# Nine q blocks turned between the layers' groups instead of on TensorE, half of the score columns, and 18 decoding steps moved to GpSimd

## The chip, the cores and the metric

The kernel runs on one core of a Trainium2 chip. The metric is the device time of one launch in microseconds, as the median of several runs. The engines that compute are TensorE (matrix products and transposes, in the profile PE for the products and PEld for the loads of its weights), VectorE (DVE), ScalarE (ACT) and GpSimd (POOL). SyncE (SP) issues nearly all DMAs. Each engine works through its own instructions in order.

## What is computed

The reference, cut to what matters: an attention over 49 agents, and behind it two feed-forward layers, for 12480 tokens of 128 channels.

```python
def sm(a, b):
    s = scale * (a @ b.transpose(0, 2, 1))
    s = s - s.max(-1, keepdims=True)
    e = np.exp(s)
    return e / (e.sum(-1, keepdims=True) + 1e-09)
agent_v = sm(agents, k) @ v              # 49 x 128
x = sm(q, agents) @ agent_v              # 12480 x 128
h = x @ w_in;   g = h * (1.0 / (1.0 + np.exp(-h)));   x = g @ w_out      # 128 -> 2048 -> 128
h = x @ w2_in;  g = h * np.cos(h);                    x = g @ w2_out     # 128 -> 2048 -> 128
```

q, k, v and the agents are float32. The four weights are float64 and are read as pairs of 32-bit words, from which the kernel builds a high and a low part of each weight itself.

## The kernel before

The program has two parts.

**The attention** works on 13 blocks of k, q and v (12 of 1024 tokens, one of 192). A long string, `ORDER`, lists its steps one by one; each engine takes its own instructions in that order, so the string fixes the order on every engine. A step's name is two letters and a block. For a k block: `kT` (eight 128x128 transposes on TensorE), `kX` (copy by ScalarE), `kS` (scores, with TensorE's columns split into two halves of 64), `kM` (a maximum on VectorE). For a v block: `vt` (transposes of the scores), `vc` (copy), `va` (product with v, columns split again). For a q block: `qT`, `qX` (turned, copied), `qS` (eight score products, one for each 128 tokens), `qM`, `qB`, `qE`, `qZ`, `qR` (maximum, subtraction, exponential, sum, reciprocal), `qN` (GpSimd multiplies by the reciprocal), `qP`, `qK`, `qL` (GpSimd packs the probabilities, 49 columns each, as high part, low part and 30 columns more of the high part into 128 columns), `qt` (TensorE turns the packed tile, four 128x128 transposes for each half block) and `qk` (ScalarE copies the turned half block into its place `pT`). The right operand of `qS` holds the 49 agents twice, so each product has 98 columns, of which the next product overwrites the second 49.

Beside this run the 16 pieces of the weights' decoding. For each piece: `dA` and `dH` on ScalarE, and `d0`, `d1`, `d2`, `d3`, `d4`, `dL` on VectorE. `d4` subtracts the high part from the value, `dL` adds the rest and writes the low part; both read two 128x512 tiles in SBUF. A second string, `LOADS`, gives the order in which SyncE issues the loads of k, q, v and the weights' pieces; a load is issued when a buffer of its kind is free (five for k and q, three for v, three for w).

At the end of the attention, when the last `va` is done, `c0` to `c6`, `cA`, `ch`, `cw`, `cP`, `cl`, `cH` and `cs` multiply the agents' values into the first layer's weights, so that the layers read the turned probabilities `pT` directly. A third string, `FIRST`, orders what is left over beside the first five groups of the first layer (`LR`, `Lh`, `La`, `Lg`, `Ll`, `Ly`). In it `wy8` is eight products on TensorE whose result is not used.

**The layers** work on 25 tiles of 512 tokens (the last three are shorter), and on four groups of 512 hidden units for each tile. One turn of the loop over `g` issues group `g` of the first layer and group `q = g - 5` of the second. On TensorE a group takes the products of `L1_rest` and `L1_h` (hidden units), `L1_y`, `L2_h` and `L2_y`. VectorE takes `L1_lo`, `L2_r`, `L2_g` and `L2_hi` in each turn; in addition `L1_end_b` where `g % 4` is 0 and the output's transpose `L2_end` where it is 2. GpSimd takes `L2_lo` alone. `L1_rest_in` loads 19 rows of `pT` four times over, one turn of four ahead of their use.

Of the kernel before, what the change touches and what calls it, by code (L numbers as in the profile page):

```python
# [31 lines left out]
LINE = 32  # L32

# [24 lines left out]
cH2 qN11 LR0 cl1 Lh0.0 cs3 dA14 Lh0.1 qP11 cH1 La0.0 qK11 qL11 cw1 cs2 Lg0.0 qK12 cs1 qL12 La0.1 wy8 qt12.0  # L58
Ll0.0 LR1 Lg0.1 Lh1.0 d213 Lh1.1 d014 Ly0.0 La1.0 Ll0.1 Lg1.0 d114 LR2 Lh2.0 La1.1 d313 Lh2.1 Ll1.0 Ly0.1 dH14
Lg1.1 d214 Ly1.0 d413 La2.0 Ll1.1 qk12.0 Lg2.0 LR3 d314 Lh3.0 Ly1.1 La2.1 Ll2.0 Lg2.1 d115 Ly2.0 La3.0 Ll2.1  # L60
Lh3.1 Lg3.0 qt11.0 dL13 d414 LR4 La3.1 Lh4.0 Ll3.0 Ly2.1 dH15 Lg3.1 d215 Lh4.1 d315 Ly3.0 La4.0 Ll3.1 Lg4.0 d415
Ly3.1 La4.1 Ll4.0 dL15 qk11.0 Le3 qt11.1 Lf3 qk11.1 dL14
# [3 lines left out]
w0 k0 k1 k2 w1 k3 k4 k5 w2 q0 k6 w3 k7 k8 w4 q1 k10 w5 k9 q2 k12 k11 w6 v1 q3 v0 q4 w7 q5 q10 q6 w8 q8 q7 v3 q9  # L66
w9 w10 v2 v4 w11 v5 q12 v6 q11 w12 v9 v7 v10 w13 v8 v11 v12 w15 w14
# [4 lines left out]
def agent_attention_moe_moe_kernel(ctx, tc, q, k, v, agents, w_in, w_out, w2_in, w2_out, out):  # L72
# [17 lines left out]
    agT = const.tile([128, 2, NA], F32, name="agT")  # L90
# [10 lines left out]
    const.tile([128, LINE - 8], F32, name="fill")  # L101
# [46 lines left out]

    whole = ctx.enter_context(ExitStack())
# [16 lines left out]
    if True:  # L166
# [27 lines left out]
        def load(key, S):  # L194
# [53 lines left out]
        for j in range(2):  # L248
            nc.vector.tensor_copy(out=agT[:, j, :], in_=pa[:, :NA])
# [122 lines left out]
        def qS(S):  # L372
# [4 lines left out]
            ag2 = agT.rearrange("p j a -> p (j a)")  # L377
# [570 lines left out]
```

## Time and profile before

| | |
|---|---|
| median of 3 runs | 1080.2 us (1079.47 to 1080.25) |
| span of the profiled execution, first to last instruction | 1076.8 us |
| the profiled execution's own time | not listed apart; the runs' median lies 3.4 us above its span |
| busy: PE, PEld, DVE, ACT, POOL | 1065.2, 841.2, 964.1, 909.8, 504.0 us |
| mean granted TensorE clock | 0.999 |

The page divides the span into 40 slices and gives for each engine the busy share of a slice. Busy time of PE is not PE at its peak: matrix products are pipelined and their ends are modelled. Which work sets the end is read from the chain that ended last, stretch by stretch; what an engine that is not in the chain has left is read from the windows.

### The profile page before, as it was taken

The numbers are of one execution on the slowest core, as the hardware profiler recorded it, in microseconds if no ns is written. First come the engines' busy times: TensorE is split into PE (matmuls) and PEld (weight loads), VectorE is DVE, ScalarE is ACT, GpSimd is POOL, SyncE is SP. The second block draws the span as 40 slices with busy tenths as digits, with TensorE's granted clock in tenths as the row PEclk, the third lists the DMA queues.
The fourth block names the chain that finished last, engine by engine and source line by source line (L and its number), as shares of the span: only waits on it lengthen the run. The fifth ranks groups of instructions, "written<-read, shape, count | busy, mean of one in ns | idle before, by whom it ended". The sixth has DMA issues, their size and how long they took to land.

```text
span 1076.8 us, 14174 instructions
## 1 busy us (share of the span) xinstructions
PE 1065.2 (99%) x5267; PEld 841.2 (78%) x5267; DVE 964.1 (90%) x1067; ACT 909.8 (84%) x972; POOL 504.0 (47%) x264
## 2 busy tenths in 40 slices
PE   9999999999999999999999999999999999999997
PEld 5897777777777777777777777777777777788996
DVE  7877999989999999999989998999999999999897
ACT  5888988888888888888888888888888888888876
POOL 0445044554455445544554455445544554455555
PEclk9999999999999999999999999999999999999999
DMA  9963000000000000000000000000000000000000
GB/s 345 344 226 125 9 6 11 6 16 13 4 16 16 1 17 16 1 16 17 10 6 16 12 5 16 13 4 16 17 1 16 16 1 15 15 11 5 12 9 15
DMA packets 66221, 38.68 MB, mean 36 GB/s; under 512 B 52523, under 2 KB 57184, under 8 KB 66152
## 3 DMA queue, kind: packets, MB, share of 16 engines
q1 hardware_dynamic: 65352, 37.68, 11.5%
q8 instruction: 41, 0.67, 0.3%
q14 instruction: 28, 0.23, 0.1%
q10 hardware_dynamic: 800, 0.10, 0.1%
HBM read 27.58 MB, written 6.39 MB: 32 GB/s over the span
## 4 chain that ended last, share of the span: by engine, by line
PE 95%; DVE 2%; ACT 1%; POOL 1%; DMA 1%; issue 1%; SPq 0%; POOLq 0%; DVEq 0%; ACTq 0%
PE y L733 16%; PE y L737 16%; PE y L734 16%; PE h L701 10%; PE h L775 8%; PE h L777 8%; PE h L776 8%; PE h L689 4%; PE h L267 2%; PE h L379 2%; PE h L303 1%; PE y L366 1%; PE y L440 1%; POOL g2l L834 1%; DMA kraw<-in_k_dram 1%; DVE g L816 1%
## 5 line engine op out<-in xcount | busy, mean ns | idle before, releaser
L834 POOL TENSOR_TENSOR g2l<-g,g2h 128x1024 fp32r<-128x1024 f32 (+2 forms) x200 | 465.5, 2349 | 498.7 <-DVE g1l L724 489.0
L799 DVE SCALAR_TENSOR_TENSOR n<-n,h 128x1024 f32<-128x1024 int32 (+3 forms) x202 | 239.0, 1184 | 63.9 <-ACT n L789 50.8
L789 ACT ACTIVATE n<-h,quarter 128x1024 int32<-128x1024 f32 (+3 forms) x202 | 219.8, 1088 | 88.7 <-PE h L777 88.6
L724 DVE TENSOR_TENSOR g1l<-g,g1h 128x1024 fp32r<-128x1024 f32 (+2 forms) x200 | 239.7, 1199 | 9.7 <-ACT g1h L716 4.1
L816 DVE TENSOR_TENSOR g<-n,h 128x1024 f32<-128x1024 f32 (+3 forms) x202 | 238.0, 1179 | 4.0 <-ACT n L808 0.7
L709 ACT ACTIVATE g<-h 128x1024 f32<-128x1024 f32 (+2 forms) x200 | 199.4, 997 | 36.2 <-PE h L701 36.0
L808 ACT ACTIVATE n<-n,halfpi 128x1024 f32<-128x1024 f32 (+3 forms) x202 | 225.6, 1119 | 0.8 <-DVE n L799 0.8
L716 ACT CAST g1h<-g 128x1024 fp32r<-128x1024 f32 (+2 forms) x200 | 204.9, 1025 | 3.2
L825 DVE CAST g2h<-g 128x1024 fp32r<-128x1024 f32 (+2 forms) x196 | 155.5, 794 | 7.5
L733 PE MATMUL y<-g1h,o1h 128*128 128x512 f32 (+2 forms) x400 | 156.4, 391 | 0.1
L733 PE MATMUL y<-g2h,o2h 128*128 128x512 f32 (+2 forms) x400 | 154.9, 387 | 1.1 <-DVE o L856 0.9
L775 PE MATMUL h<-x2h,i2h 128*128 128x512 f32 (+2 forms) x400 | 154.2, 386 | 1.0 <-DVE g L816 1.0
L734 PE MATMUL y<-g2h,o2l 128*128 128x512 f32 (+2 forms) x400 | 154.5, 386 | 0.0
L734 PE MATMUL y<-g1h,o1l 128*128 128x512 f32 (+2 forms) x400 | 154.0, 385 | 0.0
L777 PE MATMUL h<-x2l,i2h 128*128 128x512 f32 (+2 forms) x400 | 153.9, 385 | 0.0
L776 PE MATMUL h<-x2h,i2l 128*128 128x512 f32 (+2 forms) x400 | 153.9, 385 | 0.0
L701 PE MATMUL h<-pT,w2h 128*128 128x512 f32 (+2 forms) x400 | 132.3, 413 | 0.0
L737 PE MATMUL y<-g2l,o2h 128*128 128x512 f32 (+2 forms) x400 | 122.3, 387 | 1.9 <-POOL g2l L834 1.9
L737 PE MATMUL y<-g1l,o1h 128*128 128x512 f32 (+2 forms) x400 | 121.2, 384 | 0.0
L733 PEld LDWEIGHTS y<-g1h,o1h 128*128 128x128 f32 x400 | 75.1, 188 | 21.1 <-DVE x2l L762 7.8
L701 PEld LDWEIGHTS h<-pT,w2h 128*128 128x128 f32 x400 | 67.3, 188 | 30.9 <-issue 23.9
L737 PEld LDWEIGHTS y<-g2l,o2h 128*128 128x128 f32 x400 | 74.9, 188 | 17.7 <-POOL g2l L834 3.1
(140 smaller groups left out, 1092.5 us busy)
## 6 DMA issues: line engine op xcount, KB each, us to landing
qraw<-in_q_dram SPq DMA_DIRECT2D x12, 512.0 KB
vraw<-in_v_dram SPq DMA_DIRECT2D x12, 512.0 KB
kraw<-in_k_dram SPq DMA_DIRECT2D x11, 512.0 KB
out_dram<-o SPq DMA_DIRECT2D x88, 64.0 KB
wraw<-in_moe_w_in_dram SPq DMA_DIRECT2D x8, 512.0 KB
wraw<-in_moe_w_out_dram SPq DMA_DIRECT2D x8, 512.0 KB
x<-pT SPq DMA_DIRECT2D x88, 38.0 KB
kraw<-in_k_dram SPq DMA_DIRECT2D x2, 256.0 KB
```

The source lines that it names most:

```text
L701: nc.tensor.matmul(out=h1s[g, k][:, j, :toks(t)], lhsT=w2h[:, 128 * c:128 * c + 128], rhs=x, start=False, stop=True)
L724: i = v.tensor_tensor(out=gl, in0=f, in1=b32(gh), op=ALU.subtract)
L733: nc.tensor.matmul(out=y, lhsT=wh[:, c, :], rhs=gh[:, j, :], start=(c == 0), stop=False)
L734: nc.tensor.matmul(out=y, lhsT=wl[:, c, :], rhs=gh[:, j, :], start=False, stop=False)
L737: nc.tensor.matmul(out=y, lhsT=wh[:, c, :], rhs=gl[:, j, :], start=False, stop=(c == NCH - 1))
L775: nc.tensor.matmul(out=y, lhsT=i2h[:, c, :], rhs=xh, start=True, stop=False)
L776: nc.tensor.matmul(out=y, lhsT=i2l[:, c, :], rhs=xh, start=False, stop=False)
L777: nc.tensor.matmul(out=y, lhsT=i2h[:, c, :], rhs=xl, start=False, stop=True)
L799: v.scalar_tensor_tensor(out=b32(n)[:, p], in0=n[:, p], scalar=-2.0 * PI, in1=h2s[g, k][:, p], op0=ALU.mult, op1=ALU.add)
L808: sc.activation(out=r[:, p], in_=r[:, p], func=AF.Sin, bias=halfpi)
L816: v.tensor_tensor(out=f[:, p], in0=r[:, p], in1=h[:, p], op=ALU.mult)
L834: i = (v if (g, k) == (NG - 1, 1) else gp).tensor_tensor(out=gl[:, p], in0=f[:, p], in1=b32(gh)[:, p], op=ALU.subtract)
```

## The change

Five things are changed.

1. In the attention, q blocks 2 to 10 end with `qN`, which now writes its result into a place of its own, `stash` (free places of later `pT` tiles). Their steps `qP`, `qK`, `qL`, `qt` and `qk` are gone.
2. For these blocks the layers' loop does the same work two tiles ahead of use, for each tile of 512 tokens: GpSimd packs half a block (`P_hi` where `g % 4` is 0, `P_lo` where it is 1), VectorE transposes its 32x32 squares (`P_turn`, where `g % 4` is 3), and five DMAs put the squares in their places by way of a buffer in HBM. The tokens of these tiles come in another sequence, so the q loads of the nine blocks become four DMAs of 32 partitions each, and the output DMAs write accordingly.
3. `qS` multiplies 64 tokens at a time by the 49 agents, held once: 16 products of 49 columns on the two halves of TensorE's columns in place of 8 of 98.
4. Ten `d4` (written `e4`) and eight `dL` (`eL`) go from VectorE to GpSimd.
5. `ORDER`, `FIRST` and `LOADS` are new throughout; `wy8` is gone, and the loads begin with k block 6.

```diff
+LATE = (2, 3, 4, 5, 6, 7, 8, 9, 10)
+HOME = {2: 8, 3: 9, 4: 10, 5: 0, 6: 1, 7: 2, 8: 3, 9: 4, 10: 0}
+STASH = {2: (2, 0), 5: (2, 1), 3: (3, 0), 6: (3, 1), 4: (4, 0), 7: (4, 1), 8: (5, 0), 9: (5, 1), 10: (6, 0)}
+STAGE = 7
...
-dA0 d00 d10 kT0 wm3 d20 dH0 d30 kX0 d40 kT1 dL0 kS0 kX1 kT2 kM0 dA1 kS1 kX2 d01 d11 kT3 kM1 dH1 kS2 d21 kX3 d31
...
+kT6 dA0 kX6 d00 d10 kT0 wm3 d20 dH0 kS6 d30 kX0 e40 kT10 kM6 dL0 kS0 kX10 kT8 dA1 kM0 d01 kS10 kX8 d11 d21 kT1 dH1 d31
...
-    agT = const.tile([128, 2, NA], F32, name="agT")
+    agT = const.tile([128, NA], F32, name="agT")
...
+            if key == "q" and S in LATE:
+                src = q[0, blocks[S][0]:blocks[S][0] + 1024, :].rearrange("(x i a s) c -> a i x (s c)", x=2, i=32, s=4)
+                for a in range(4):
+                    nc.sync.dma_start(
+                        out=t[32 * a:32 * a + 32].rearrange("i (x s) c -> i x (s c)", x=2), in_=src[a]
+                    )
+                return t
...
-                nc.tensor.matmul(
-                    out=ps[:p, NA * i:NA * i + 2 * NA], lhsT=xt[:, i // h, p * (i % h):p * (i % h) + p], rhs=ag2,
-                    start=True, stop=True,
-                )
+                for x in range(0, p, 64):
+                    w = min(64, p - x)
+                    at = p * (i % h) + x
+                    nc.tensor.matmul(
+                        out=ps[x:x + w, NA * i:NA * i + NA], lhsT=xt[:, i // h, at:at + w], rhs=agT,
+                        start=True, stop=True, tile_position=(0, x),
+                    )
...
-            nc.gpsimd.tensor_tensor(out=e, in0=e, in1=z.unsqueeze(2).to_broadcast([p, n, NA]), op=ALU.mult)
+            nc.gpsimd.tensor_tensor(out=stash(S) if S in LATE else e, in0=e, in1=z.unsqueeze(2).to_broadcast([p, n, NA]), op=ALU.mult)
...
+            e4=lambda S: d4(S, nc.gpsimd), eL=lambda S: dL(S, nc.gpsimd),
...
+        def P_hi(t, after_op):
+            if not half(t):
+                return
+            e, pk = late_in(t)
+            i = gp.tensor_copy(out=pk[:, :, 0:NA], in_=e)
+            tc.add_manual_dep(i.ins, after_op.ins.name, AFTER, reason="one at a time on the port to SBUF")
+            gp.tensor_copy(out=pk[:, :, 2 * NA:128], in_=e[:, :, 0:MORE])
+
+        def P_lo(t, after_op):
+            if not half(t):
+                return
+            e, pk = late_in(t)
+            i = gp.tensor_tensor(out=pk[:, :, NA:2 * NA], in0=e, in1=b32(pk)[:, :, 0:NA], op=ALU.subtract)
+            tc.add_manual_dep(i.ins, after_op.ins.name, AFTER, reason="one at a time on the port to SBUF")
+
+        def P_turn(t):
+            if not half(t):
+                return
+            v.transpose(
+                out=b32(stage(1)).rearrange("p (x s i) -> p s x i", x=4, i=32),
+                in_=b32(stage(0)).rearrange("p (s x i) -> p s x i", x=4, i=32),
+            )
+            d = scratch.tile([128, 4, 128], F32, tag="turned", name="turned")
+            nc.sync.dma_start(out=d, in_=b32(stage(1)).rearrange("p (x c) -> p x c", x=4))
+            for x in range(4):
+                nc.sync.dma_start(
+                    out=b32(pT(WIDE * t, WIDE))[32 * x:32 * x + 32, :].rearrange("j (a c) -> j a c", a=4),
+                    in_=d[:, x, :].rearrange("(a j) c -> j a c", j=32),
+                )
...
-            L2_hi(q - 1, 0)
+            hi = L2_hi(q - 1, 0)
             L1_h(g, 0)
+            if g % 4 == 0:
+                P_hi(g // 4 + 2, hi)
+            if g % 4 == 1:
+                P_lo(g // 4 + 2, hi)
...
             L2_n(q, 1)
+            if g % 4 == 3:
+                P_turn(g // 4 + 2)
             L2_r(q, 0)
```

What this moves on the engines is read from the instructions in order. On TensorE, in the middle of the attention, the order before was this (L267 transposes of k and q, L346 of the scores, L440 of the packed probabilities, L379 the q scores, L366 the products with v; x8 counts instructions):

```order
L346 MATMUL h_929<-ident,sT 128x128 x4
L379 MATMUL h_937<-agT,xT 128x98 x8
L440 MATMUL y_959<-ident,pk 128x128 x4
L379 MATMUL h_964<-agT,xT 128x98 x8
L440 MATMUL y_984<-ident,pk 128x128 x4
L346 MATMUL h_992<-ident,sT 128x128 x4
L366 MATMUL y_194<-vraw,eT 49x128 x16
L440 MATMUL y_1030<-ident,pk 128x128 x4
```

On the same engine at the corresponding place of the changed kernel (L287, L366, L401 and L386 are now the transposes of q, those of the scores, the q scores and the products with v):

```order
L366 MATMUL h_971<-ident,sT 128x128 x4
L287 MATMUL h_979<-ident,qraw 128x128 x8
L401 MATMUL h_994<-agT,xT 64x49 x16
L386 MATMUL y_195<-vraw,eT 49x128 x8
L401 MATMUL h_1033<-agT,xT 64x49 x16
L386 MATMUL y_195<-vraw,eT 49x128 x8
L401 MATMUL h_1067<-agT,xT 64x49 x16
L366 MATMUL h_1088<-ident,sT 128x128 x4
```

The transposes of packed probabilities are gone between the score products, these are 16 small products for a block instead of 8, and they stand directly beside products with v, which split the columns in the same way.

On VectorE in the layers, where `g % 4` goes from 2 to 3, the order before was this (L816 `L2_g`, L856 `L2_end`, L825 `L2_hi`, L724 `L1_lo`, L799 `L2_r`):

```order
L816 TENSOR_TENSOR g_2514<-n,h_2478 128x1024
L856 STREAM_TRANSPOSE o<-y_2204 128x512
L825 CAST g2h<-g_2514 128x1024
L816 TENSOR_TENSOR g_2548<-n,h_2478 128x1024
L724 TENSOR_TENSOR g1l<-g_2512,g1h 128x1024
L825 CAST g2h<-g_2548 128x1024
L724 TENSOR_TENSOR g1l<-g_2550,g1h 128x1024
L799 SCALAR_TENSOR_TENSOR n<-n,h_2554 128x1024
```

And on VectorE in the changed kernel (L839, L880, L848, L747 and L822 are the same steps):

```order
L839 TENSOR_TENSOR g_2150<-n,h 128x1024
L880 STREAM_TRANSPOSE o<-y_1836 128x512
L848 CAST g2h<-g_2150 128x1024
L839 TENSOR_TENSOR g_2184<-n,h_2114 128x1024
L747 TENSOR_TENSOR g1l<-g_2148,g1h 128x1024
L848 CAST g2h<-g_2184 128x1024
L747 TENSOR_TENSOR g1l<-g_2186,g1h 128x1024
L912 STREAM_TRANSPOSE stage<-stage 128x4x4x32
L822 SCALAR_TENSOR_TENSOR n<-n,h_2190 128x1024
```

One transpose of a 128x512 tile has come in ahead of the first `L2_r` of the turn; all else on VectorE stands as it stood.

## Rows read from the trace of the kernel before

**Rows 1.** The page: the span, the loads.
```profile
span 1076.8 us, 14174 instructions
...
HBM read 27.58 MB, written 6.39 MB: 32 GB/s over the span
```

**Rows 2.** The windows: stretch, length, busy time of each engine, granted clock, DMA share, GB/s.
```profile
core 0: us, PE busy (x) PEld busy (x) DVE busy (x) ACT busy (x) POOL busy (x), PEclk, DMA share, GB/s
0.00:10.00 10.00, 8.02 (x35) 4.94 (x36) 4.77 (x24) 3.62 (x5) 0.96 (x10) 1.00 0.74 253
10.00:50.00 40.00, 40.00 (x287) 27.84 (x286) 33.34 (x79) 29.42 (x41) 8.89 (x12) 1.00 1.02 382
50.00:94.00 44.00, 44.00 (x474) 40.12 (x474) 34.98 (x74) 37.25 (x69) 24.03 (x35) 1.00 0.59 203
94.00:105.00 11.00, 9.87 (x58) 7.56 (x58) 8.67 (x21) 9.57 (x19) 2.53 (x5) 1.00 0.31 109
105.00:130.00 25.00, 24.59 (x126) 18.57 (x127) 23.43 (x32) 24.24 (x29) 2.05 (x5) 1.00 0.03 12
200.00:1000.00 800.00, 799.91 (x3618) 625.53 (x3618) 728.35 (x700) 686.72 (x680) 393.38 (x166) 1.00 0.05 11
```

**Rows 3.** The chain that ended last, 0 to 170 us: start, length, what.
```profile
22.73 1.76 PE h L379 x16
...
69.74 0.44 PE y L440 x4
...
70.61 1.89 PE y L366 x32
72.50 0.59 PE y L440 x4
...
75.28 1.01 PE y L366 x16
...
92.75 1.26 PE y L366 x20
...
105.26 2.04 PE y L275 x16
```

**Rows 4.** Timelines of narrow stretches near 10.5 us, TensorE's weight loads, then its products.
```profile
10.46 0.14 PEld L303 LDWEIGHTS h<-xT,agk 128*64 128x64 f32 x2 [0.17 <-issue]
...
10.51 0.14 PEld L303 LDWEIGHTS h<-xT,agk 128*64 128x64 f32 x2
...
10.46 0.65 PE L303 MATMUL h<-xT,agk 128*64 128x512 f32 x2
```

**Rows 5.** Groups by line: count, busy us, mean ns of one, idle before.
```profile
L856 DVE STREAM_TRANSPOSE o<-y 128x512 f32<-128x512 f32 (+2 forms) x25 | 17.4, 696 | 0.7 <-PE y L737 0.7
...
L445 ACT CAST pT<-y 128x512 fp32r<-128x512 f32 (+1 forms) x25 | 14.4, 577 | 4.2 <-PE y L440 4.0
...
L429 POOL TENSOR_TENSOR pk<-e,pk 128x392 fp32r<-128x392 f32 (+1 forms) x13 | 12.0, 924 | 0.0
...
L493 DVE TENSOR_TENSOR a<-a,w2h 128x512 f32<-128x512 f32 x4 | 2.7, 685 | 0.0
...
L608 ACT ACT_TABLE_LOAD x1 | 1.3, 1283 | 0.0
```

**Rows 6.** Timeline of VectorE, 55 to 61 us: the same step twice.
```profile
55.14 1.33 DVE L485 SCALAR_TENSOR_TENSOR m<-wraw,m 128x512 f32<-128x512 uint32 x1
...
60.93 0.64 DVE L485 SCALAR_TENSOR_TENSOR m<-wraw,m 128x512 f32<-128x512 uint32 x1
```

**Rows 7.** Timeline of TensorE: the second layer's first product.
```profile
128.37 0.39 PE L775 MATMUL h<-x2h,i2h 128*128 128x512 f32 x1
```

**Rows 8.** Timeline of VectorE in the layers: `L2_r`, twice in a turn.
```profile
305.79 2.59 DVE L799 SCALAR_TENSOR_TENSOR n<-n,h 128x1024 f32<-128x1024 int32 x2 [0.55 <-ACT n L789]
```

**Rows 9.** Timelines of SyncE's queue and of TensorE: `x` issued and used.
```profile
98.37 2.42 SPq L676 DMA_DIRECT2D x<-pT  x4
...
102.69 0.49 PE L689 MATMUL h<-x,w 19*128 19x512 f32 x1 [0.20 <-DMA x<-pT]
```

More of the change, by code (lines that the diff above doesn't have):

```diff
@@ new lines @@
+e41 kS8 kM10 kX1 qT0 dA2 kM8 eL1 d02 kS1 qX0 d12 d22 kT9 dH2 d32 e42 qS0 kM1 kX9 kT5 dA3 qM0 eL2 qB0 kS9 kX5 d03 d13
+kT11 qE0 d23 dH3 d33 kS5 kX11 qZ0 qT1 qR0 kM5 qN0 kM9 kT2 qX1 qP0 d43 kS11 qK0 dL3 qL0 dA4 qS1 kM11 kX2 d04 qt0.1 qM1
+kT7 qk0.1 qB1 kT4 d14 qE1 kX7 d24 kS2 d34 dA5 qZ1 kS7 kX4 qR1 d05 qN1 qt0.0 kM2 dH4 kT3 kM7 qP1 qk0.0 qT2 d44 qK1 kX3
+qL1 dL4 kS4 dA6 d15 qt1.1 kM4 qX2 kS3 d25 dA7 d06 qS2 d16 dH5 d35 qk1.1 e45 kT12 qT4 kX12 qM2 dH6 qT5 qB2 qX4 eL5 d46
+qt1.0 kM3 qE2 qT3 qk1.0 qZ2 kS12 qR2 qS4 d26 qN2 qX3 kM12 x0 d07 x1 qX5 qM4 qS3 x2 dA8 qB4 qT6 qM3 qE4 x3 qB3 qX6 qS5
@@ L55 @@
+vt11 qM11 eL10 qX12 va10 vc11 qB11 qR10 qE11 d211 qS12 qN10 vt8 dA13 qM12 qB12 d311 vt12 vc8 va11 e412 qZ11 vc12 qE12
+st qZ12 va8 qR12 d013 qN12 dL11 qP12 qK12 va12 qL12 c0 c1 qt12.0 d212 c2 qk12.0 d312 c4 c3 c6 eL12 c5 cA0 dA15 qR11
+d113 d015 dH13 qN11 d115 cP0 ch0 d215 qP11 dH15 cA1 cw0 ri0 e413 cl0 d415 cH0 cs0 cP1 dA14 qK11 d213 qL11 cP3 ch1 d313
+cl1 cP2 cw1 eL13 cl3 cH1
 """
 FIRST = """
-cH2 qN11 LR0 cl1 Lh0.0 cs3 dA14 Lh0.1 qP11 cH1 La0.0 qK11 qL11 cw1 cs2 Lg0.0 qK12 cs1 qL12 La0.1 wy8 qt12.0
@@ L59 @@
[L59 to L62, printed above, removed]
+LR0 cl2 cH3 Lh0.0 cs2 Lh0.1 La0.0 cH2 Lg0.0 cs1 cs3 La0.1 LR1 Ll0.0 Lh1.0 Lg0.1 Lh1.1 qt11.1 d315 Ly0.0 La1.0 Ll0.1
@@ L68 @@
+q10 w9 v4 v2 v5 w10 w11 w12 v7 v6 v9 w13 v10 v11 v8 v12 w15 w14
 """
@@ L100, in agent_attention_moe_moe_kernel @@
     halfpi = const.tile([128, 1], F32, name="halfpi")
-    const.tile([128, LINE - 8], F32, name="fill")
+    const.tile([128, LINE + 40], F32, name="fill")
     turned = {}
@@ L110, in pT, with stash, stage @@
         if j not in turned:
-            turned[j] = home(j, "pT", F32R, 2048)
+            turned[j] = home(HOME.get(j, j), "pT", F32R, 2048)
         return turned[j][:, begin - 1024 * j:begin - 1024 * j + width]
+    stashes, stages = {}, []
+    def stash(S):
+        slot, i = STASH[S]
+        if slot not in stashes:
+            stashes[slot] = home(slot, "stash", F32)
+        return stashes[slot][:, 512 * i:512 * i + 8 * NA].rearrange("p (s a) -> p s a", a=NA)
+    def stage(i):
+        if not stages:
+            stages.append(home(STAGE, "stage", F32R))
+        return stages[0][:, 512 * i:512 * i + 512]
     w2h = wts.tile([128, DFF], F32R, name="w2h")
@@ L247, in agent_attention_moe_moe_kernel @@
         nc.vector.tensor_copy(out=agk[:, 0:NA], in_=pa[:, :NA])
-        for j in range(2):
-            nc.vector.tensor_copy(out=agT[:, j, :], in_=pa[:, :NA])
+        nc.vector.tensor_copy(out=agT, in_=pa[:, :NA])
         for x in (0, 64):
@@ L824, in L2_hi @@
             for p in parts(g):
-                (sc.copy if k and g + LAG >= NG else v.tensor_copy)(out=gh[:, p], in_=g2s[g, k][0][:, p])
+                i = (sc.copy if k and g + LAG >= NG else v.tensor_copy)(out=gh[:, p], in_=g2s[g, k][0][:, p])
             g2s[g, k].append(gh)
+            return i
         def L2_lo(g, k):
@@ L857, in L2_end, with half, late_in @@
             for cb in range(4):
+                o_dram = out[span(t), 32 * cb:32 * cb + 32]
                 (nc.scalar if t == 24 and cb % 2 else nc.sync).dma_start(
-                    out=out[span(t), 32 * cb:32 * cb + 32].rearrange("(b i) j -> i b j", i=32),
+                    out=o_dram.rearrange("(i b) j -> i b j" if half(t) else "(b i) j -> i b j", i=32),
                     in_=o[32 * cb:32 * cb + 32],
+                )
+        def half(t):
+            return t // 2 in LATE and t < 2 * (NS - 2)
+        def late_in(t):
+            return stash(t // 2)[:, 4 * (t % 2):4 * (t % 2) + 4, :], stage(0).rearrange("p (s a) -> p s a", a=128)
+        def P_hi(t, after_op):
[24 more added lines that the diff above has]
+                    in_=d[:, x, :].rearrange("(a j) c -> j a c", j=32),
                 )
```

58 lines of the change are left out of this document (24 added, 34 removed).

## The prediction

> **What bounds the kernel now.** I read the windows first. From 10 us on TensorE is busy all the time: 40.00 of 40, then 44.00 of 44 us, and in the layers 799.91 of 800 [rows 2]. Its granted clock is 1.00 in every stretch, the 2.4 GHz level [rows 2]. The next view is the chain: up to 94.0 us (92.75 + 1.26) it is a string of TensorE groups with hardly anything between them [rows 3]. So in the attention every microsecond taken from TensorE moves the end, until another engine or the loads take over, and in the layers nothing is gained by anything that isn't TensorE's. The reader is to see how much the others have left. Up to 94 us VectorE is busy 4.77 + 33.34 + 34.98 = 73.1 us and ScalarE 70.3 us; between 10 and 50 us the DMAs are full (share 1.02, 382 GB/s) and then they are not (0.59) [rows 2]. In the stretch of the first layer groups, 105 to 130 us, ScalarE is the busiest beside TensorE, 24.24 of 25 us [rows 2].
>
> **The transposes that leave TensorE.** Nine blocks times two halves are 18 groups of four. A group takes 0.44 us, or 0.59 where it follows a product with split columns [rows 3]. That 0.15 belongs to the change between full and split columns and not to the transposes. Counted along `ORDER`, TensorE changes between the two 48 times before and 48 times after, because the new score products, now split too, stand beside other split groups. I take the plain 0.44: **-7.9 us** for certain, as TensorE's work. The Trainium skill (TensorEngine Tiling, Key Properties) says that switching the tiling mode drains TensorE; the trace agrees, with 0.59 against 0.44, and it speaks against half columns in `qS`. Were each of the twelve score groups alone, that would be 24 changes more, 3.6 us, and the gain 4.3; by the count of the order it stays 7.9.
>
> **The score products.** A block's eight products are 16 records (two passes each), 1.76 us, 0.11 each [rows 3], with 98 columns. The new form, 64 tokens by 49 columns, isn't in the trace. Its nearest rows are `kS` and `va`, which split the columns likewise. In `kS` the loads of the weights come two at a time: the first pair starts at 10.46, the next at 10.51 (0.05 to 0.06 later), and two products start together at 10.46 and run side by side [rows 4]. In `va`, 16 records more cost 1.89 - 1.01 = 0.88 us [rows 3], a pair in 0.11, with 128 streaming columns. The new block is 32 records, 16 pairs. If a pair is paced by its weight loads of 64 columns, it takes 0.055 and the block 0.88; if pairs take what `va`'s do, 0.11 and 1.76, no gain. With 49 streaming columns of `va`'s 128 the streaming itself would need only 0.04, so I take 0.055: 12 blocks x 0.88 = **-10.6 us**, bounds 0 and -10.6.
>
> **The other engines in the attention.** Up to the last `va` ScalarE has 15 copies of 0.577 fewer and one table load of 1.28 more [rows 5]: 70.3 - 8.7 + 1.3 = 62.9 us. VectorE has 12 subtractions and sums of 0.685 [rows 5] fewer there, and 0.7 of small steps more: 65.6 us. GpSimd gets 15 steps on 128x512 tiles. By its own subtraction (0.924 for 392 columns [rows 5]) such a step is about 1.2 us, 18 us in all, against packing work that leaves it; it was busy 34 of 94 us [rows 2]. TensorE's 94.0 shrink to 94.0 - 18.5 = 75.5 us. In this VectorE would be 87% busy (78% before), ScalarE 83% (75%). In the layers VectorE runs at 728.35 of 800, 91%, and TensorE doesn't wait [rows 2], but there the work repeats; here I take **+4 us** of new waits, between 0 and 10.
>
> **The joint.** From the last `va` (94.0) to the second layer's first product (128.37 [rows 7]) 34.4 us pass. `wy8` is 2.04 us of the chain there [rows 3], but ScalarE is full from 105 us on [rows 2], and whether TensorE fills or waits meanwhile is all the same. What ScalarE loses is a table load (1.28, now earlier) and one or two copies. I take **-2 us**; the bounds are 0 (the chain of small steps stays as long) and -4 (`wy8` counts in full as well).
>
> **The layers.** 18 tiles get a transpose on VectorE, 0.70 by `L2_end`'s, which reads PSUM and writes plainly [rows 5]; the strided form isn't in the trace, 0.6 to 1.4. It stands ahead of `L2_r`, where VectorE waits 0.55 us for ScalarE in each turn [rows 8]. A turn is about (1076.8 - 105) / 100 = 9.7 us, of which VectorE has 9%, 0.87 us, free [rows 2]. In other turns of four it already takes `L2_end` or `L1_end_b` of about the same length, and TensorE loses 0.09 us in 800 [rows 2]. GpSimd gets three small steps a tile, each up to half of 0.924, in turns of which it has half free (393 of 800 busy [rows 2]). The DMAs have five turns, some 48 us, until the tile is used: one round from issue to use is 98.37 + 2.42 to 102.69, 1.9 us after the last of four issues [rows 9], and here there are three rounds, the last ones in a queue that nothing hurries. If that cover were gone, each tile would wait several us. I take **+1 us**, bounds 0 and 5.
>
> **Sum.** 1076.8 - 7.9 - 10.6 + 4 - 2 + 1 = 1061.3 us of span. The runs' median is 3.4 above the span before, so **1064.7 us**, 1.4% faster. With all terms at their good end it is 1058, with them at their bad end (score products as before, waits 10, layers 5) 1087.
>
> **Rivals.**
> *The pairs don't close up.* Each score product waits for its own weights as `va`'s pairs do, 0.11. For it speaks that no row has products that short in a row, and 16 instructions must be issued in 0.88 us; against it the weight loads 0.05 apart. The attention shrinks by 7.9 only, with waits of 2: 1080.2 - 7.9 + 2 - 2 + 1 = 1073.
> *Something else takes over in the attention.* GpSimd's steps hold up VectorE: the same step took 1.33 us at 55.14, while GpSimd multiplied, and 0.64 at 60.93 [rows 6]. If each of the 15 steps up to the last `va` costs VectorE that 0.69, it has 65.6 + 10.4 = 76.0 us of work from 5 us on, and the last `va` can't come before 81. Or the loads: 27.58 MB [rows 1] less the last two weight pieces (1.05) at 382 GB/s [rows 2] are 69.4 us without a gap, so `va` can't end much before 74, and the buffers don't let the loads run freely. Either gives 6 to 9 us of waits in place of 4: 1067 to 1070, with both 1074. The Trainium skill (SBUF — State Buffer, Who interferes with whom) says that a VectorE instruction with two inputs in SBUF and a GpSimd one that reads SBUF exclude each other, the later blocked to the end. The trace agrees with a case like that at 55.14; by the rule a whole 1.2 us could be lost at each step, and the sum would be 8 us worse still.
> *The layers pay (slower).* Place: VectorE in the turns with `P_turn`. If the transpose (0.70) and the time in which GpSimd's three steps hold VectorE (up to 1.4) come through to TensorE in full, 18 x 2.1 = 38 us are lost, and the kernel takes 1064.7 - 1 + 38 = 1102. It decides from (1080.2 - 1063.7) / 18 = 0.92 us a tile. Against it: the 0.55 us of idle just there, and the other turns, which carry as much.
> *It doesn't do what it says.* The packed work must leave TensorE, so an unchanged time would need a loss of some 16 us elsewhere, for example a load order in which the first products stand still; k block 6 is now first and whole, where the first k load was in halves.
>
> **How the numbers follow.** The forecast, 1059 to 1069 us, gets 0.55, the open pairs 0.14, the attention held by another engine 0.17, the layers 0.08, the rest 0.06. The forecast's 1064.5 is the time that I give. To 8 in 10 belong the forecast and the first two rivals, less their ends: 1058 to 1077. About 0.2%, 2.2 us, is what a measurement of this kernel can tell from no change. Faster is the forecast and both of those rivals, with a part of the rest: 0.87; within 0.2% 0.04; slower 0.09.
>
> **What would show it.** Right: no `pk` transposes for nine blocks in the attention; a score block of about 0.9 us in the chain; the last `va` near 79 us; PE at 800 of 800 in the layers with VectorE near 93%; a strided transpose near 0.7. Wrong: score blocks of 1.76; waits of TensorE for kraw, qraw or vraw, or for ScalarE's xT, in sum above 8 us; waits of L1_h or L2_y on VectorE in one turn of four; a granted clock below 1.00.

## The result and the profile after

The changed kernel takes **1084.7 us** (median of 4 runs, 1084.5 to 1085.9), the kernel before, on the same chip, 1079.8 us. The ratio is 1.0053 (95% interval 1.0039 to 1.0067): 0.5% slower. The forecast was 1.4% faster, so it was wrong by 20 us and in sign.

The windows of the changed kernel, the same stretches as in [rows 2] (busy time of PE, PEld, DVE, ACT, POOL, then granted clock, DMA share, GB/s):

```profile
10.00:50.00 40.00, 34.93 (x351) 23.06 (x349) 33.02 (x72) 26.89 (x37) 17.09 (x16) 1.00 0.98 319
50.00:94.00 44.00, 35.86 (x538) 31.79 (x536) 37.91 (x68) 31.91 (x58) 20.27 (x18) 0.92 0.79 250
94.00:105.00 11.00, 8.14 (x49) 7.14 (x46) 8.40 (x17) 6.41 (x16) 8.54 (x10) 0.84 0.31 108
105.00:130.00 25.00, 21.90 (x96) 15.32 (x95) 19.90 (x28) 20.59 (x23) 1.29 (x1) 0.93 0.04 14
200.00:1000.00 800.00, 799.91 (x3615) 624.20 (x3614) 736.87 (x716) 686.55 (x679) 411.06 (x213) 1.00 0.09 22
```

TensorE, which waited for nothing before, is now idle 13.2 of the 84 us from 10 to 94. VectorE is little busier (70.9 us against 68.3), and the DMAs move 319 GB/s in the first stretch instead of 382, at about the same share (0.98 and 1.02). From 50 us on the granted clock is no longer 1.00: TensorE, left idle, falls in places to the 1.2 GHz level (0.50 from 74.5 to 76.5 us). The layers are as before, 799.91 of 800.

The chain that ended last in the changed kernel, some of its longest pieces between 18 and 105 us (start, length, what):

```profile
32.27 9.19 DMA wraw<-in_moe_w_out_dram
...
48.17 7.31 DMA qraw<-in_q_dram
...
71.59 1.63 DVE m L507
...
74.52 1.95 PE h L401 x32
...
98.04 3.00 PE y L583 x12
```

In [rows 3] the attention was a string of TensorE's groups. Here it has two loads of 9.19 and 7.31 us in it, and ahead of them and behind them VectorE's steps of the decoding, 1.63 us for one that took 0.64 [rows 6]. The last two rows are TensorE's own: a block of score products takes 1.95 us at the low clock. At full clock it comes near the forecast, which the timeline of TensorE shows at 19 us: the next group starts 1.07 us later, and the forecast's 0.88 and 0.15 for a change of columns are 1.03.

```profile
19.27 1.14 PE L401 MATMUL h<-agT,xT 128*64 128x49 f32 x32
20.34 1.09 PE L287 MATMUL h<-ident,kraw 128*128 128x128 f32 x8
```

Two landmarks divide the time into attention, joint and layers: the last product with v and the second layer's first product. These are groups with count, min/mean/max ns, first and last start. First the products with v of the kernel before, whose first product of layer 2 is in [rows 7]:

```profile
L366 PE MATMUL y<-vraw,eT x148: 271/273/313, 70.5 to 93.7; 128*49 128x128 f32 x144, 96*49 96x128 f32 x4
```

And both of the changed kernel:

```profile
L386 PE MATMUL y<-vraw,eT x132: 270/273/313, 70.5 to 94.2; 128*49 128x128 f32 x128, 96*49 96x128 f32 x4
...
L798 PE MATMUL h<-x2h,i2h x8: 387/446/628, 133.1 to 145.0; 128*128 128x512 f32 x8
```

| | attention: last product with v starts | joint, up to the first product of layer 2 | from there to the end | span |
|---|---|---|---|---|
| before | 93.7 | 34.7 | 948.4 | 1076.8 |
| forecast of the change in it | -14.5 | -2 | +1 | -15.5 |
| after | 94.2 (+0.5) | 38.9 (+4.2) | 949.6 (+1.2) | 1082.7 (+5.9) |

So 15 us are missing in the attention and 6 in the joint. The layers agree with the forecast in their number, but not in its reason, as shown further down.

### The profile page after: what moved, and what is told of

It reads as the page before. It is cut to its first block, busy times and chain, and to the rows that moved or that the text cites. A ratio compares the mean times of both kernels' runs of the same rounds, so it can differ in the third digit from the quotient of the medians.

```text
span 1082.7 us, 14639 instructions
## 1 busy us (share of the span) xinstructions
PE 1054.1 (97%) x5375; PEld 827.9 (76%) x5375; DVE 973.5 (90%) x1066; ACT 900.9 (83%) x954; POOL 535.1 (49%) x309
## 4 chain that ended last, share of the span: by engine, by line
PE 90%; DVE 4%; DMA 2%; ACT 1%; issue 1%; POOL 1%; SPq 1%; POOLq 0%; DVEq 0%; ACTq 0%
PE y L756 17%; PE y L757 16%; PE y L760 16%; PE h L724 10%; PE h L798 8%; PE h L800 8%; PE h L799 8%; PE h L712 4%; DMA wraw<-in_moe_w_out_dram 1%; PE h L287 1%; DMA qraw<-in_q_dram 1%; DVE a L491 0%; SPq L225 0%; DVE m L507 0%; POOL g2l L858 0%
## 5 line engine op out<-in xcount | busy, mean ns | idle before, releaser
L822 DVE SCALAR_TENSOR_TENSOR n<-n,h 128x1024 f32<-128x1024 int32 (+3 forms) x202 | 238.9, 1184 | 56.7 <-ACT n L812 43.8
L747 DVE TENSOR_TENSOR g1l<-g,g1h 128x1024 fp32r<-128x1024 f32 (+2 forms) x200 | 239.6, 1198 | 14.1 <-ACT g1h L739 9.2
L839 DVE TENSOR_TENSOR g<-n,h 128x1024 f32<-128x1024 f32 (+3 forms) x202 | 238.0, 1179 | 3.5 <-issue 0.3
L732 ACT ACTIVATE g<-h 128x1024 f32<-128x1024 f32 (+2 forms) x200 | 199.3, 997 | 40.2 <-PE h L724 39.7
L848 DVE CAST g2h<-g 128x1024 fp32r<-128x1024 f32 (+2 forms) x196 | 152.8, 780 | 7.5
L798 PE MATMUL h<-x2h,i2h 128*128 128x512 f32 (+2 forms) x400 | 154.6, 387 | 0.8 <-DVE g L839 0.8
L799 PE MATMUL h<-x2h,i2l 128*128 128x512 f32 (+2 forms) x400 | 154.3, 386 | 0.0
L724 PE MATMUL h<-pT,w2h 128*128 128x512 f32 (+2 forms) x400 | 132.0, 412 | 0.0
L724 PEld LDWEIGHTS h<-pT,w2h 128*128 128x128 f32 x400 | 67.5, 188 | 30.5 <-issue 23.2
```

The source lines that it names most:

```text
L724: nc.tensor.matmul(out=h1s[g, k][:, j, :toks(t)], lhsT=w2h[:, 128 * c:128 * c + 128], rhs=x, start=False, stop=True)
L747: i = v.tensor_tensor(out=gl, in0=f, in1=b32(gh), op=ALU.subtract)
L798: nc.tensor.matmul(out=y, lhsT=i2h[:, c, :], rhs=xh, start=True, stop=False)
L799: nc.tensor.matmul(out=y, lhsT=i2l[:, c, :], rhs=xh, start=False, stop=False)
L822: v.scalar_tensor_tensor(out=b32(n)[:, p], in0=n[:, p], scalar=-2.0 * PI, in1=h2s[g, k][:, p], op0=ALU.mult, op1=ALU.add)
L839: v.tensor_tensor(out=f[:, p], in0=r[:, p], in1=h[:, p], op=ALU.mult)
```

## The experiments

Theory 1: the q loads of the nine blocks, now four DMAs of 32 partitions each, use the DMAs badly; they come late, TensorE waits, and its clock falls. Theory 2: GpSimd's 18 steps of the decoding hold VectorE up, so that nothing is relieved. Each experiment is compared with the kernel before on its own chip; all times are medians. No experiment leaves out a part of the computation. A trace is of a single execution.

**The loads whole.** The changed kernel, with each late block loaded by one DMA of 128 partitions as before; the transpose in the layers puts the tokens in their places instead.

```diff
-            if key == "q" and S in LATE:
-                src = q[0, blocks[S][0]:blocks[S][0] + 1024, :].rearrange("(x i a s) c -> a i x (s c)", x=2, i=32, s=4)
-                for a in range(4):
...
-                out=b32(stage(1)).rearrange("p (x s i) -> p s x i", x=4, i=32),
+                out=b32(stage(1)).rearrange("p (x i s) -> p s x i", x=4, i=32),
```

> The changed kernel, with the q loads of the nine blocks whole again (one DMA over 128 partitions in place of four over 32 partitions). So that it can be, VectorE's transpose in the layers writes every fourth element, which puts the tokens of a tile in their own sequence, and the output DMAs are the ordinary ones. Theory 1 (the loads in quarters use the DMA engines badly, the loads come late, TensorE waits and its clock falls): between 30 and 60 us the DMAs move 350 GB/s or more where the changed kernel had about 260; the last product with v ends at 78 to 84 us instead of about 93; the time is 1064 to 1071 us. Theory 2 (GpSimd's decoding steps hold VectorE up, and the loads only come late because buffers come free late): 1080 us or more, the last product with v after 90 us.

Measured 1079.2 us, ratio 0.9995 (0.9984 to 1.0005): the loss is gone, but the forecast gain is not there. Both theories missed: the last product with v starts at 87.5 us, between the two, and from 30 to 60 us the DMAs move 342, 318 and 324 GB/s. The form of the loads is one cause and not the whole.

**All decoding on VectorE.** The changed kernel, loads in quarters.

```diff
-            e4=lambda S: d4(S, nc.gpsimd), eL=lambda S: dL(S, nc.gpsimd),
+            e4=d4, eL=dL,
```

> The changed kernel, with all 32 differences and sums of the decoding on VectorE again and the loads in quarters as they are. Theory 1: at most 4 us better, 1080 to 1086 us, the DMAs between 30 and 60 us still at 240 to 280 GB/s. Theory 2: 1066 to 1074 us, since the attention runs without GpSimd's holds.

Measured 1084.4 us, 1.0044 (1.0024 to 1.0064), not to be told from the changed kernel. With late loads no effect of who decodes can be seen.

**Quarters in the kernel before.** Nothing changed but these loads.

```diff
+            if key == "q" and 2 <= S <= 10:
+                for a in range(4):
+                    ps = slice(32 * a, 32 * a + 32)
+                    nc.sync.dma_start(out=dst[ps], in_=src[ps])
+                return t
```

> The kernel before, with only the q loads of blocks 2 to 10 in four DMAs of 32 partitions each; tokens and all else as before. Theory 1: the nine loads take about 2.6 us of the DMA engines each in place of 1.35 (128 KB pieces at 200 GB/s), 11 us more in all, of which part is hidden because the DMAs had 40% free from 50 us on: 1083 to 1092 us, with less than 300 GB/s between 30 and 60 us. Theory 2: no change, 1079 to 1081 us.

Measured 1087.3 us, 1.009 (1.0056 to 1.0125): the loads alone cost the kernel before at least as much as the whole change does (0.9% and 0.53%, the intervals just overlap).

**Four transfers of all partitions.** As the last one, but each transfer has all 128 partitions and a quarter of the rows.

```diff
-                    ps = slice(32 * a, 32 * a + 32)
-                    nc.sync.dma_start(out=dst[ps], in_=src[ps])
+                    ss = slice(2 * (a % 2), 2 * (a % 2) + 2)
+                    nc.sync.dma_start(out=dst[:, a // 2:a // 2 + 1, ss, :], in_=src[:, a // 2:a // 2 + 1, ss, :])
```

> The kernel before with the q loads of blocks 2 to 10 in four transfers each, as in the run with quarters (ratio 1.009), but each of all 128 partitions with 2 of 8 rows, in pieces of 1 KB instead of 2 KB. Theory 'transfers of 32 partitions are slow': the rate stays at that of before and the time at 1078 to 1081. Rival 'four transfers instead of one are slow, by their number or by short pieces': 1085 to 1092.

Measured 1079.5 us, 1.0006 (0.9997 to 1.0015): no loss. It is the 32 partitions, not the number of transfers or the length of their pieces, which were 1 KB here and 2 KB there. The windows of the two kernels, 32 partitions first (its trace is of the slowest of four runs, 1094.6 us):

```profile
30.00:40.00 10.00, 9.51 (x73) 7.24 (x72) 7.82 (x19) 5.94 (x10) 6.15 (x8) 1.00 1.07 236
40.00:50.00 10.00, 4.47 (x34) 2.89 (x32) 4.69 (x10) 4.30 (x7) 0.00 (x0) 0.89 1.07 187
```

```profile
30.00:40.00 10.00, 10.00 (x79) 7.87 (x77) 7.93 (x21) 7.50 (x11) 6.07 (x8) 1.00 1.03 355
40.00:50.00 10.00, 10.00 (x85) 8.60 (x84) 8.17 (x22) 7.65 (x13) 2.86 (x5) 1.00 0.95 294
```

The share says that the DMA engines are busy in both, 1.07 and 1.03 or 0.95; what they move is 236 and 187 GB/s in the one, 355 and 294 in the other. And TensorE is busy 4.47 of 10 us in the one, all the time in the other. The changed kernel, which loads by 32 partitions too, moves 245 and 234 GB/s in the same stretches. The Trainium skill (SBUF — State Buffer, Door 1: The DMA port swizzle) says that 32 neighbouring partitions reach only half of the ports by which DMAs write to SBUF. The Trainium skill (SBUF — State Buffer, Can I just issue two DMAs to hit both halves?) says that two transfers at once hardly make up for it. The traces agree, with two thirds of the rate (236 to 355, 187 to 294) for four transfers in a row.

**Both mended.** The changed kernel with whole loads and all decoding on VectorE: the first two edits together.

> The changed kernel with its late q blocks loaded whole (time 1079.2, ratio 0.9995) and, besides, all decoding on VectorE. Theory 'GpSimd's 18 steps hold VectorE up': VectorE runs at its own durations again and TensorE's waits go: 1074 to 1077. Rival 'VectorE's own work in this order is the bound, and GpSimd's steps relieve it': 18 steps of 0.65 us come back to VectorE, which was busy 66.7 of the 70 us from 20 to 90: 1082 to 1088. If both are about as large: 1078 to 1081.

Measured 1076.3 us, 0.9974 (0.9963 to 0.9985). Against the run with whole loads alone 0.2% faster, so GpSimd's steps do harm, about 2 us, once the loads are in time; the two intervals just touch. The groups of VectorE's decoding steps from 10 to 94 us, with GpSimd's steps beside them (whole loads alone) and without (both mended):

```profile
L484 DVE SCALAR_TENSOR_TENSOR a<-wraw,a 128x512 uint32<-128x512 uint32 x14 | 13.3, 952 | 0.3
...
L500 DVE SCALAR_TENSOR_TENSOR m<-wraw,m 128x512 f32<-128x512 uint32 x12 | 11.3, 940 | 0.3
```

```profile
L484 DVE SCALAR_TENSOR_TENSOR a<-wraw,a 128x512 uint32<-128x512 uint32 x14 | 11.0, 783 | 0.2
...
L500 DVE SCALAR_TENSOR_TENSOR m<-wraw,m 128x512 f32<-128x512 uint32 x12 | 8.7, 728 | 0.3
```

The same steps are 170 to 210 ns longer beside GpSimd's. On GpSimd itself a step has a mean of 1.26 to 1.61 us, by group, for the 0.69 that it takes on VectorE [rows 5]:

```profile
L513 POOL TENSOR_TENSOR i2l<-m,a 128x512 fp32r<-128x512 f32 x2 | 3.2, 1606 | 0.2
...
L513 POOL TENSOR_TENSOR o2l<-m,a 128x512 fp32r<-128x512 f32 x1 | 1.3, 1264 | 0.0
```

**GpSimd's steps in the order of before.** The kernel before, with the same ten `d4` and eight `dL` written `e4` and `eL`.

> The kernel before, with only those 18 steps of the decoding moved to GpSimd that the change moves, in the order of before. Theory 'GpSimd's steps stretch VectorE's by as much as they take from it': 1079 to 1082, within 0.2% of before, with VectorE's steps of 0.43 to 0.69 us at 1.2 to 1.7 us beside them. Rival 'the steps are a relief': TensorE was busy all the time from 20 to 90 us in this order, so that only the joint from 94 us on can gain: 1077 to 1079. Rival 'they hold TensorE up': 1083 to 1088.

Measured 1080.0 us, 1.001 (1.0001 to 1.0019): no relief here either, hardly a loss.

**Half columns alone.** The kernel before, with the score products of the change. `agT` is 49 floats smaller there, and a filler tile makes up for it; in a first run the filler was one float longer than in the change.

```diff
-    const.tile([128, LINE - 8], F32, name="fill")
+    const.tile([128, LINE + 41], F32, name="fill")
...
+                for x in range(0, p, 64):
+                    w = min(64, p - x)
+                    at = p * (i % h) + x
+                    nc.tensor.matmul(
+                        out=ps[x:x + w, NA * i:NA * i + NA], lhsT=xt[:, i // h, at:at + w], rhs=agT,
+                        start=True, stop=True, tile_position=(0, x),
+                    )
```

> The kernel before, with only the q scores in half columns (16 products of 49 columns instead of 8 of 98, agents held once). If pairs are paced by their weight loads (0.055 us), a block's group takes 0.88 us plus about 0.3 for two changes of the column split: 12 x (1.76 - 0.88) - 24 x 0.15 = 7.0 us less work on TensorE, 1072 to 1077 us as far as the other engines keep up with the old order. If pairs take 0.11 us: 3.6 us slower, 1083 us.

Measured 1080.8 us, 1.0018 (1.0007 to 1.0028). The second layer's first product came at 123.2 us, 5.2 us sooner than before, and the end came no sooner: the layers had become slower. The second run has `LINE + 40`, as the change has, and nothing else is different.

> The kernel before with half-column q scores, as in the first such run (span 1077.0 us, time 1080.8), but with the filler tile one float smaller, so that all tiles behind it stand at the addresses that they have before. In the first run the first products of layer 2 came 5.2 us sooner than before and then each full block took 39.40 us instead of 39.17. Theory 'the shifted addresses slow the layers': a block takes 39.17 us again, the 5.2 us last to the end: span 1071 to 1072, time 1074 to 1075. Rival 'what starts sooner is given back by the layers whatever the addresses' (VectorE or ScalarE set the pace): a block stays at 39.4 us, time 1080 to 1081.

Measured 1075.3 us, 0.996 (0.9946 to 0.9974). From the second layer's first product to the end it takes 948.5 us; the first run took 953.8, the kernel before 948.4. By plain count it is the slow run's filler that makes up for the 49 floats exactly, so the places of the tiles must be rounded in some way. No run shows the addresses; I suppose that the one float moves the tiles behind it by 32 bytes, since the next run, with a filler 32 bytes longer, takes the same time in the layers.

**Addresses alone.** The kernel before with the filler 8 floats longer.

```diff
-    const.tile([128, LINE - 8], F32, name="fill")
+    const.tile([128, LINE], F32, name="fill")
```

> The kernel before with nothing changed but the filler tile, 8 floats (32 bytes a partition) larger, so that the tiles behind it stand 32 bytes further on. Theory 'the shifted addresses slow the layers': a full block takes 39.40 us instead of 39.17, 21 blocks and the shorter ones about 5 us: 1084 to 1086. Rival 'addresses don't matter': 1079 to 1081.

Measured 1084.5 us, 1.0046 (1.0033 to 1.006), and 953.7 us from the second layer's first product on. ScalarE's timelines show the same copy at the end of layer 1, 18 blocks apart, before and with the longer filler:

```profile
199.58 0.59 ACT L754 CAST x2h<-y 128x512 fp32r<-128x512 f32 x1 [0.24 <-PE y L737]
...
904.72 0.59 ACT L754 CAST x2h<-y 128x512 fp32r<-128x512 f32 x1 [0.24 <-PE y L737]
```

```profile
199.98 0.59 ACT L754 CAST x2h<-y 128x512 fp32r<-128x512 f32 x1 [0.24 <-PE y L737]
...
909.34 0.59 ACT L754 CAST x2h<-y 128x512 fp32r<-128x512 f32 x1 [0.24 <-PE y L737]
```

A block takes (904.72 - 199.58) / 18 = 39.17 us and (909.34 - 199.98) / 18 = 39.41. Without this pair the half columns would have been put down as worthless.

**The clock in the joint.** Both mended, with 16 dummy products in the wait ahead of the second group of layer 1.

```diff
+        def wz(n):
+            unit(banky("y1")[:, 0:128], n)
...
-LR0 cl2 cH3 Lh0.0 cs2 Lh0.1 La0.0 cH2 Lg0.0 cs1 cs3 La0.1 LR1 Ll0.0 Lh1.0 Lg0.1 Lh1.1 qt11.1 d315 Ly0.0 La1.0 Ll0.1
+LR0 cl2 cH3 Lh0.0 cs2 Lh0.1 wz16 La0.0 cH2 Lg0.0 cs1 cs3 La0.1 LR1 Ll0.0 Lh1.0 Lg0.1 Lh1.1 qt11.1 d315 Ly0.0 La1.0 Ll0.1
```

> The changed kernel with late q blocks loaded whole and all decoding on VectorE (time 1076.3, ratio 0.9974), and with 16 dummy products of 128 columns (about 2 us at full clock) on TensorE in the wait of 2.49 us ahead of the second group of layer 1, after which the granted clock was 0.66 from 100 to 110 us. Theory 'the low clock in the joint costs time': products there go back from 0.43 to 0.23 us each, the first full block ends 1 to 3 us sooner: 1073.5 to 1075.5. Rival 'VectorE's decoding steps, 7 to 9 of each 10 us there, set the pace and the clock is hidden': 1076 to 1077.

Measured 1076.2 us, 0.9972 (0.9961 to 0.9984), the same. The windows without and with the dummy products:

```profile
100.00:110.00 10.00, 8.01 (x28) 5.63 (x29) 7.68 (x11) 7.14 (x8) 0.00 (x0) 0.66 0.03 11
```

```profile
100.00:110.00 10.00, 10.00 (x62) 8.21 (x61) 7.80 (x11) 7.86 (x8) 0.00 (x0) 0.91 0.03 10
```

The clock is mended, 0.66 to 0.91, and nothing is gained: the second layer's first product starts at 126.2 us, without the dummy products at 126.0. What holds the joint is in the chain of the kernel without them:

```profile
96.76 0.69 DVE m L500
...
97.91 0.60 DVE o2l L513
...
101.14 0.71 DVE w2h L611
...
101.99 0.80 PE h L705 x4
```

These are VectorE's last steps of the decoding and of `cs`, done nearly without a gap up to 101.85; only then TensorE goes on.

**The order of before.** Both mended (the half columns stay), but with `ORDER`, `FIRST` and `LOADS` of before, less `qP`, `qK`, `qL`, `qt` and `qk` of the nine blocks.

> The order of instructions and of loads of before, without the late blocks' transposes and copies (they are turned in the layers as in the change, their loads whole), with half-column q scores and all decoding on VectorE. Theory 'the order written for the change, in which VectorE is late from 20 us on, costs the rest': TensorE's sum of -7.9 and -5 us shows better here: 1068 to 1073. Rival 'VectorE's and ScalarE's work and the loads bound the attention whatever the order, as soon as TensorE has 13 us less to do': 1074 to 1077, as with the change's own order.

Measured 1072.2 us, 0.9938 (0.9924 to 0.9952), the fastest of all; the traced execution took 1075.2, 3 us over the median. Its chain and the waits of the load queue (waited for: us in all, times, longest):

```profile
43.07 7.97 DMA qraw<-in_q_dram
...
62.45 7.40 DMA vraw<-in_v_dram
...
71.01 7.83 DMA vraw<-in_v_dram
```

```profile
SPq L217 <- DVE m L504: 16.5, 4, 8.0
```

Here the loads end last. The queue stands up to 8.0 us before a w load whose buffer VectorE has not yet freed, and the v loads stand behind it. But the same wait is as long in the kernel before, where TensorE is busy all the time:

```profile
SPq L199 <- DVE m L485: 17.1, 4, 8.2
```

**Two v loads ahead of two w loads** in that kernel.

```diff
-w9 w10 v2 v4 w11 v5 q12 v6 q11 w12 v9 v7 v10 w13 v8 v11 v12 w15 w14
+v2 v4 w9 w10 w11 v5 q12 v6 q11 w12 v9 v7 v10 w13 v8 v11 v12 w15 w14
```

> The kernel with the order of before, late turning, half-column q scores and whole loads (time 1072.2, ratio 0.9938), with one edit in the order of its loads: two v loads stand ahead of two w loads that wait 8 us on the load queue for VectorE to free their buffers (46.0 to 54.1 us), while the transfers fall to 104 GB/s from 50 to 60 us and TensorE later waits for v at 62 to 70 and 71 to 79 us. Theory 'the v loads stuck behind the w loads are what bounds this order now': the v loads land some 2 to 5 us sooner, and the time is 1067 to 1071. Rival 'the v buffers are freed no sooner, or the w loads are then late for VectorE': 1071 to 1075.

Measured 1077.3 us, 0.9988 (0.9979 to 0.9997): slower than without the edit, and slower than the rival expected as well. The theory falls.

```profile
SPq L228 <- PE y L383: 23.9, 7, 10.3
```

Now the queue stands up to 10.3 us before a v load, whose buffer the products with v have not yet freed. Both kinds of buffers are full at this time. Whether yet another sequence of these loads would mend that was not tried.

## Why the prediction was wrong

The kernels stand in a row in which each differs from the next by one thing. The steps add up to the whole change, but each has about +-0.2% by the two intervals.

| from | to | what is added | ratio of the second to before | step |
|---|---|---|---|---|
| before | half columns | score products | 0.9960 | -0.40% |
| half columns | order of before | late turning, loads whole | 0.9938 | -0.22% |
| order of before | both mended | `ORDER`, `FIRST`, `LOADS` of the change | 0.9974 | +0.36% |
| both mended | loads whole | GpSimd's 18 steps | 0.9995 | +0.21% |
| loads whole | after | q loads by 32 partitions | 1.0053 | +0.58% |

The two landmarks of the result, read in the traces of the same kernels, tell where each step lies. Shown are the lines of the two orders, the order of before first:

```profile
L383 PE MATMUL y<-vraw,eT x196: 270/273/451, 55.9 to 89.2; 128*49 128x128 f32 x192, 96*49 96x128 f32 x4
...
L794 PE MATMUL h<-x2h,i2h x400: 334/389/498, 124.8 to 1060.8; 128*128 128x512 f32 x118, 128*128 128x416 f32 x10, 128*128 128x384 f32 x6
```

```profile
L379 PE MATMUL y<-vraw,eT x196: 271/273/312, 52.9 to 85.8; 128*49 128x128 f32 x192, 96*49 96x128 f32 x4
...
L791 PE MATMUL h<-x2h,i2h x400: 333/389/500, 126.0 to 1061.9; 128*128 128x512 f32 x118, 128*128 128x416 f32 x10, 128*128 128x384 f32 x6
```

| traced execution | attention | joint | to the end |
|---|---|---|---|
| before | 93.7 | 34.7 | 948.4 |
| half columns | 90.9 | 34.7 | 948.5 |
| order of before | 89.2 | 35.6 | 948.6 |
| both mended | 85.8 | 40.2 | 948.5 |
| loads whole | 87.5 | 39.0 | 949.6 |
| after | 94.2 | 38.9 | 949.6 |

**The step that failed** is the term of +4 us for new waits, bounds 0 to 10. With the two savings as they were forecast, 18.5 us, an attention that is 0.5 us longer means some 19 us of waits and low clock, 15 more than the term had. The term was made from the room that VectorE, ScalarE and GpSimd would have left on average, and the loads stood in it only as a rival at the 382 GB/s of [rows 2]. Three things make up the 15.

The first is the form of the q loads. The four DMAs of 32 partitions, which the text on the change names, were never priced, as transfers of another form. They run at about 190 to 240 GB/s, and this costs 0.58% here and 0.9% in the order of before; in the table it is 6.7 us of the attention (94.2 to 87.5). It alone puts the time above that of before. The second is GpSimd's steps, 1.7 us (87.5 to 85.8). The third is what is left with both mended, 6.6 us over the 79.2 that the forecast had. There VectorE, which was to be 87% busy, is busy 48.76 of 50 us from 20 to 70 us, and its steps and two loads (q at 34, v at 75 us) make up most of the chain. The windows of before and of both mended:

```profile
20.00:70.00 50.00, 50.00 (x427) 41.68 (x426) 41.97 (x94) 40.07 (x64) 19.10 (x25) 1.00 0.81 295
```

```profile
20.00:70.00 50.00, 45.11 (x611) 36.39 (x612) 48.76 (x105) 40.67 (x65) 14.52 (x16) 0.97 0.95 337
```

Only GpSimd's steps were tried to relieve VectorE there, and they did not, so how this third part divides between VectorE and the loads is not shown.

**The transposes, -7.9 us.** They left TensorE as said, but of the 7.9 only 0.22%, 2.4 us, shows, even with whole loads and the better order, and this is hardly more than the noise. TensorE was the bound only by a little: the loads take over at 43, 62 and 71 us, as the rival had it, "the buffers don't let the loads run freely".

**The score products, -10.6 us.** The pairs close up; the rival that they don't is out. Behind split columns a block takes 0.92 us (both mended), near the forecast's 0.88. Behind full columns it takes 1.07, and the full group after it 1.02 instead of 0.87. The rows of both mended, of before (whose block of 1.76 at 22.73 is in [rows 3]) and of half columns:

```profile
44.74 0.92 PE h L394 x32
```

```profile
24.49 0.87 PE h L267 x8
```

```profile
22.35 1.07 PE h L380 x32
23.42 1.02 PE h L266 x8
```

So a block that stands alone, as most do in the order of before, saves 1.76 + 0.87 - 1.07 - 1.02 = 0.54 us, 6.5 us for twelve. Of that 0.40%, 4.3 us, reach the end.

**GpSimd's steps.** The rival was right in its mechanism and half wrong in its price: 1.2 us a step on GpSimd was low (1.26 to 1.61), and the cost is 0.21%, 2.3 us, not 6 to 9. It was no relief in any of the three pairs of kernels. The rule of the Trainium skill that the prediction named (SBUF — State Buffer, Who interferes with whom) agrees in its direction. The 8 us that the prediction made of it were far too many: VectorE's steps are 0.17 to 0.21 us longer in the mean, not a whole 1.2.

**The joint, -2 us,** came out at +4.2, outside its bounds of -4 to 0, and this is the second step that failed: the term counted what TensorE and ScalarE lose there and left VectorE's decoding out. In all traces the joint is 34.6 to 36.2 us in the order of before and 38.9 to 40.6 in that of the change, whoever decodes and however the q loads come. VectorE comes late to it with decoding still to do, as the chain above shows. The low clock in the joint is a follower: with it mended the time stayed.

**The layers, +1 us:** +1.2, but by luck. The reason that was given, the transpose on VectorE, costs next to nothing: from 200 us on TensorE is busy 799.91 of 800 us in both, and with all decoding on VectorE, transposes and all, this part takes 948.5 to 948.7 us, before 948.4. The +1.2 stands only in the two traces with GpSimd's steps and the order of the change. It lies in layer 2's first products, some of which take 628 ns in place of about 390 (the line of L798 above) while the granted clock is 0.83 from 140 to 150 us. The transpose on strided squares took what a plain one takes, the forecast 0.70:

```profile
L912 DVE STREAM_TRANSPOSE stage<-stage 128x512 f32<-128x512 f32 x18 | 12.7, 704 | 0.0
```

The rival on the other side, that the layers pay, did not come; the kernel ended on that side by another way.

**The 3.4 us** between span and time were partly chance of the traced execution: in each run that lists both, the time is 1.8 us above the span (1084.5 and 1082.7 after).

**Still open.** By the landmarks the whole +0.36% between the two orders lies in the joint (4.6 us longer), and the attention is even 3.4 us shorter with the order of the change. But the trace of the order of before is 3 us over its median, and the two kernels ran on different chips, so the 3.4 us may be chance. A kernel with the attention of the one order and the joint of the other was not run. And why the addresses matter (below) was seen but not explained.

## What to carry to other kernels

Price a transfer by its form and not by its bytes: when the number of partitions of a load changes, its rate is unknown until a row of that form is found, and a full DMA share with fewer GB/s is its sign. Where one engine is the bound with the loads, VectorE and ScalarE at 75 to 100% beside it, a saving on it counts in full only up to the first of them; here 7.9 + 6.5 = 14.4 us of TensorE's work taken away in the order of before gave at best 0.62%, 6.7 us. Before an edit is given up, see whether its gain was lost elsewhere: landmarks in the trace (attention 5 us sooner, layers 5 us longer) showed that, and a filler of the right length gave most of it back.

## What the runs showed of the hardware

A shift of the tiles by 32 bytes a partition costs 0.46%, nearly all of it in the layers' products that read two of the tiles, `g2h` and `g2l`. The groups from 200 to 600 us, before and with the longer filler (busy us, mean ns):

```profile
L733 PE MATMUL y<-g2h,o2h 128*128 128x512 f32 x164 | 64.3, 392 | 0.0
...
L775 PE MATMUL h<-x2h,i2h 128*128 128x512 f32 x164 | 63.9, 390 | 0.0
...
L737 PE MATMUL y<-g2l,o2h 128*128 128x512 f32 x164 | 50.8, 391 | 0.0
```

```profile
L733 PE MATMUL y<-g2h,o2h 128*128 128x512 f32 x164 | 65.0, 397 | 0.0
...
L775 PE MATMUL h<-x2h,i2h 128*128 128x512 f32 x161 | 62.8, 390 | 0.0
...
L737 PE MATMUL y<-g2l,o2h 128*128 128x512 f32 x164 | 51.5, 395 | 0.0
```

A product with `g2h` or `g2l` is 4 to 5 ns longer, one with `x2h` is not; 48 such products a block make about 0.22 us, and a block is 0.24 us longer. No busy share shows it, since TensorE is at 100% in both.
